# When and where sixteen weight tiles are decoded in a fused attention, gated MoE and channel-mixing kernel

## The chip, the cores and the metric

One core of a Trainium2 chip runs one program. The metric is the device time of one execution in microseconds (us), the median of several runs. Less is better. TensorE multiplies matrices (PE in the profile, PEld for its weight loads), VectorE (DVE), ScalarE (ACT) and GpSimd (POOL) work element by element, and SyncE (SP) issues transfers (DMAs) from one in-order queue.

## The reference

All arithmetic is float32; the weights `w_in`, `w_out`, `w_ch1`, `w_ch2` (and the small `conv_w`, `U`, `V`) arrive as float64.

```
x = attention(q, k, v, s)                 # 4 batches x 8 heads, 576 tokens, causal, exp, then P @ v
h = relu(x @ w_in)                        # 512 -> 1024, first MoE
x = (h * sigmoid(conv3(h))) @ w_out       # 1024 -> 512
u = x + (x.T @ U @ V).T                   # token mixing, rank 32
out = u + relu(u @ w_ch1) @ w_ch2         # 512 -> 2048 -> 512, second MoE
```

## The kernel before

**Arithmetic.** A float32 product is made of float32r matmuls on a high and a low part of each operand, three matmuls for one. The two big products of the second MoE use a Strassen scheme of seven products on halves (`WN`, `UN`, `VN`). The first, `u @ w_ch1`, is called the mixture here: 32 calls of `m2_in(f, g)`, where f is one of 8 pairs of row blocks and g one of 4 groups of tokens (PSUM tiles `ma`). The second, the last product of the program, is `m2_out` (tiles `my`).

**Weights.** A float64 tile of 128x512 is loaded as 512 KB into a buffer `raw` and decoded by `decode64`: one ACT instruction (line 538) and two DVE instructions (lines 545 and 554). The weights of the first MoE are done by head 11. After that two kinds of tiles go this way. `raw_w2a` are the tiles of `w_ch1`: `bring_w2a(f)` issues the loads of tiles f and f+8, `load_w2a(f)` decodes them and makes the seven high and low blocks, called W_f here, that `m2_in(f, ...)` multiplies with. `raw_w2b` are the 16 tiles of `w_ch2`: `keep_w2b` loads one, decodes it into `wf_w2b` and stores it (256 KB) to a DRAM scratch `w2b_d`, from which `load_w2b` reads it for the last product. All `raw` tiles share a ring of **two** buffers (`RINGS["w64"]`), so a load waits until the tile two before it is decoded. `wf_w2b` has a ring of two buffers too (three in the mixture), and a decode waits until the store of an earlier one has read its buffer.

**Stages.** (1) Attention over heads 0 to 31, in the loop `for h in range(NH + 1)`; from head 8 on the first MoE of the batch before is interleaved. (2) The first MoE of the last batch (`parts`), with W_0 and the u tiles prepared beside it. (3) The mixture, with W_1 to W_7 prepared about two blocks ahead. (4) The last product.

**What sets the order.** Every operation is recorded with an engine, a cost and the buffers that it reads and writes. `Plan.order` plays the program through with these costs and writes out each engine's instructions in the order in which they started there. The real engines run those orders, in order, and wait for data by semaphores. A transfer issued at t is booked to land at `max(wire, t + 1400) + bytes / 360 + 980 + slack` ns: 3.84 us later for an unhindered load of 512 KB with slack 0. If it lands later than booked, the instruction that needs it waits at the head of its engine's queue, with everything behind it.

**The 16 `keep_w2b` before:** one each at heads 13 to 17 and 23 to 27 (`W2B_AT`), where `keep_next` in the attention loop records it ahead of the parts of the first MoE; the other six in the mixture, after the calls with f = 1 and 2, g = 2 and 3, and after the first two with f = 3. Their order is tile 0, 8, 1, 9, 2, 10, and so on (`order2`). The store of a tile is recorded by the `keep_next` after it.

Of the kernel before, what the change touches and what calls it, by code (L numbers as in the profile page):

```python
# [60 lines left out]

FG = [(5, 0), (6, 0), (5, 1), (7, 0), (6, 1), (7, 1), (5, 2), (6, 2), (5, 3), (6, 3), (7, 3), (7, 2)]
EARLY2 = 8
W2B_AT = (13, 14, 15, 16, 17, 23, 24, 25, 26, 27)
OUT_AT = {0: "o11", 18: "o22", 22: "o21", 28: "o12"}
LAG2 = 6

# [3 lines left out]
WIRE = 1500  # L71
# [264 lines left out]
def tile_attention_moe_mixer(  # L336
# [14 lines left out]
    nc = tc.nc  # L351
# [13 lines left out]
    def dma(nbytes, fn, r, w):  # L365
        return plan.op("SP", 640, fn, r, w, late=nbytes / 360)
# [776 lines left out]
    def load_w2a(f, pool_):  # L1143

        blk = pool_.buf("W", [128, 2 * 7 * 256], F32R, f"W{f}")
        ws_[f] = blk

        def at(i, n, part):
            return lambda: blk[:, part * 1792 + 256 * i : part * 1792 + 256 * (i + n)]

        def keys(i, n, part):
            return [(blk, WN[j] + "hl"[part]) for j in range(i, i + n)]

        def decode(i):
            w = ring(dec, "wf", RINGS["wf"], [128, 512], F32, f"wf_w2a{f}_{i}")
            decode64(lambda: w(), [w], st["w2a", f][i], 512)
            return w

        def split(i, n, src, r):
            hi_act(at(i, n, 0), src, [r], keys(i, n, 0), 256 * n)  # L1160
            lo_dve(at(i, n, 1), src, at(i, n, 0), [r, *keys(i, n, 0)], keys(i, n, 1), 256 * n)

        def add(o, oi, x, y, op, r):
            dve(
                256,
                lambda: nc.vector.tensor_tensor(o[:, oi : oi + 256], x(), y(), op),
                r,
                [(o, oi)],
            )

        def part(t, i):
            return lambda: t[:, i : i + 256]

        wa = decode(0)
        split(0, 2, lambda: wa(), wa)
        yield
        wb = decode(1)
        split(2, 1, part(wb, 256), wb)
        yield
        sa, sb = (ring(w2a, "tt", RINGS["tt"], [128, S], F32, f"{n}_{f}") for n in ("S12", "S34"))  # L1180
        add(sa, 0, part(wb, 0), part(wb, 256), ALU.add, [wb])
        add(sa, 256, part(sa, 0), part(wa, 0), ALU.subtract, [(sa, 0), wa])
        split(3, 2, lambda: sa[:, 0:512], sa)
        yield
        add(sb, 0, part(wa, 0), part(wb, 0), ALU.subtract, [wa, wb])
        add(sb, 256, part(wa, 256), part(sa, 256), ALU.subtract, [wa, (sa, 256)])
        split(5, 2, lambda: sb[:, 0:512], sb)
        yield
# [72 lines left out]
    stores = []  # L1261

    def keep_w2b(ff):

        r = ring(dec, "raw", RINGS["w64"], [128, 512], I64, f"raw_w2b{ff}")
        dma(524288, lambda: nc.sync.dma_start(out=r(), in_=w2[ff][:, 512:]), [], [r])
        at = (w2a, "tt", RINGS["tt"], [128, S]) if st.get("mixed") else (dec, "wf", RINGS["wf"], [128, 512])
        w = ring(*at, F32, f"wf_w2b{ff}")
        decode64(lambda: w[:, :512], [w], r, 512)

        def store():
            o = dma(262144, lambda: nc.sync.dma_start(out=w2b_t[ff], in_=w[:, :512]), [w], [w2b_d[ff]])
            o.preds.add(next(x for x in reversed(plan.ops) if x.eng == "PE"))

        stores.append(store)

    def keep_next(more=True):
        while stores:
            stores.pop()()
        if order2 and more:  # L1280
            keep_w2b(order2.pop(0))

    def load_w2b(p):

        blk = w2_[p]
        r = ring(dec, "raw", RINGS["w64"], [128, 1024], F32, f"wb{p}")
        wa, wb = (Part(r, lambda t, a=a: t[:, a : a + 512], f"wb{p}_{a}") for a in (0, 512))
        for w, ff in ((wa, p), (wb, p + 8)):
            dma(262144, lambda w=w, ff=ff: nc.sync.dma_start(out=w(), in_=w2b_t[ff]), [w2b_d[ff]], [w])

        def at(i, n, part):
            return lambda: blk[:, part * 1792 + 256 * i : part * 1792 + 256 * (i + n)]

        def keys(i, n, part):
            return [(blk, VN[j] + "hl"[part]) for j in range(i, i + n)]

        def split(i, n, src, r):
            hi_act(at(i, n, 0), src, [r], keys(i, n, 0), 256 * n)
            lo_dve(at(i, n, 1), src, at(i, n, 0), [r, *keys(i, n, 0)], keys(i, n, 1), 256 * n)

        def add(o, oi, x, y, op, r):
            dve(256, lambda: nc.vector.tensor_tensor(o[:, oi : oi + 256], x(), y(), op), r, [(o, oi)])

        def part(t, i):
            return lambda: t[:, i : i + 256]

        split(0, 1, part(wa, 0), wa)
        yield
        split(1, 2, lambda: wb(), wb)
        yield  # L1310
        sa, sb = (ring(w2a, "tt", RINGS["tt"], [128, S], F32, f"{n}_b{p}") for n in ("S12", "S34"))
        add(sa, 0, part(wa, 256), part(wb, 256), ALU.add, [wa, wb])
        add(sa, 256, part(sa, 0), part(wa, 0), ALU.subtract, [(sa, 0), wa])
        split(3, 2, lambda: sa[:, 0:512], sa)
        yield
        add(sb, 0, part(wa, 0), part(wa, 256), ALU.subtract, [wa])
        add(sb, 256, part(wb, 0), part(sa, 256), ALU.subtract, [wb, (sa, 256)])
        split(5, 2, lambda: sb[:, 0:512], sb)
        yield
# [228 lines left out]
    for h in range(NH + 1):  # L1548
        b, hh = divmod(h - 1, H)
        todo = []  # L1550
        if b >= 1:
            parts = m1_parts(b - 1)
            whole = sum(w for w, t in parts)
            at, todo = 0, []
            for w, t in parts:
                if hh <= at * H / whole < hh + 1:
                    todo.append(t)
                at += w
        att_head(h)
        if h in W2B_AT or stores:  # L1560
            keep_next(h in W2B_AT)
        for n, (f, c) in enumerate(w1_jobs):
            if h == W1_AT[n]:
                load_split(w1[f], w1h[f, c], w1l[f, c], c, 512, f"w1_{f}_{c}", lo_dve, SLACK)
        if h == CW_AT:
            load_cw()
        if h == MIX_AT:
            load_mixu()
            for c in (0, HS):
                load_mixv(c)  # L1570
        for t in todo:
            t()

    w2a = Pool(plan, "w2a", "right", after=[ap.close()])

# [13 lines left out]

    st["late"] = True  # L1590

    bring_w2a(0)
    blocks = [u_block(w2a, 0)]
    steps = each(load_w2a(0, w2a), load_u(0, blocks[0])())
    parts = m1_parts(B - 1)
    for n, (w, t) in enumerate(parts):
        if n >= len(parts) // 3 and n % 2:
            next(steps, None)
        t()
# [36 lines left out]
    for dt in range(KT):  # L1636
        keep(B - 1, dt)

    m2_in(0, 2)
    m2_in(0, 3)  # L1640
    for f in (1, 2):
        bring_w2a(f + 2)
        steps = load_w2a(f + 2, pools[(f + 2) % 3])
        for g in (2, 3):
            next(steps)
            next(steps)
            m2_in(f, g)
            keep_next()
    for f in (3, 4):
        bring_w2a(f + 2)  # L1650
        steps = load_w2a(f + 2, pools[(f + 2) % 3])
        for g in range(NG):
            next(steps)
            m2_in(f, g)
            if order2 or stores:
                keep_next()
    bring_w2a(7)
    steps = load_w2a(7, pools[7 % 3])
# [36 lines left out]
    for i, (f, g) in enumerate(FG):  # L1695
        if i < 4:
            next(steps)
        m2_in(f, g)
        if f == 7 and g < 2:
            blk = (w2a, u1p)[g].buf(f"u{g}", [128, 2 * 7 * S], F32, f"w2_{g}")  # L1700
            add_w2(2 * g, blk, 0)
            add_w2(2 * g + 1, blk, 3584)
            pair(blk, 7168)
        elif f == 7:
            blk = u2p.buf(f"u{g}" + "a" * (g - 2), [128, (14 if g == 2 else 8) * S], F32, f"w2_{g}")
            add_w2(9 - g, blk, 0)
            if g == 3:
                pair(blk, 3584)
                blk = u2p.buf("u3b", [128, 6 * S], F32, "b21")
                b21 = [Cell(blk, k * NC2) for k in range(9)]  # L1710
            else:
                for k in range(5):
                    pair(blk, 3584 + 2 * k * NC2)
        elif g == 3:
            add_w2(f - 1, w_block(f, f"w2_W{f}"), 0)
        if i == 8:
            for ff in range(8):
                m2_bring(0, ff, "11")
# [114 lines left out]
```

## Time and the profile before

| | |
|---|---|
| median of 3 runs | 801.37 us (800.07 to 802.52) |
| the profiled execution | 799.74 us, span of its instructions 797.9 us |
| PE busy | 768.7 us, 96% of the span |
| DVE, ACT, POOL busy | 581.5 (73%), 526.0 (66%), 185.2 us (23%) |
| DMA | 132.84 MB, mean 166 GB/s |

PE is busy in almost every slice of the span, so time can come only from the stretches in which it sits idle or runs at a lower clock. Matmuls are pipelined, and busy time counts the overlap of two once. The time in brackets at the end of a timeline row is the idle time of that engine ahead of the instruction, with what ended it.

### The profile page before, as it was taken

How to read it: one execution, taken by the hardware profiler on the slowest of the kernel's cores; microseconds unless marked ns; L12 is line 12 of the kernel's file. 1: busy time of each engine (PE TensorE's matmuls, PEld its weight loads, DVE VectorE, ACT ScalarE, POOL GpSimd, SP SyncE). 2: the span in 40 equal slices, each digit the busy share in tenths (PEclk: the TensorE clock that was granted, in tenths of full speed). 3: DMA queues.
4: the chain of work that ended last, by engine and by line, in shares of the span. 5: the costliest groups of instructions: out<-in, count | busy, mean ns of one | idle time of the engine just before them, and what ended most of it. 6: DMA issues, size and time to landing. Idle time of an engine off the chain costs nothing.

```text
span 797.9 us, 15829 instructions
## 1 busy us (share of the span) xinstructions
PE 768.7 (96%) x5348; PEld 714.8 (90%) x5348; DVE 581.5 (73%) x1406; ACT 526.0 (66%) x1328; POOL 185.2 (23%) x291
## 2 busy tenths in 40 slices
PE   5999999899999989999999999999999999999998
PEld 3557797798889978999999999999999899999997
DVE  5987897536774458736789875567487998988983
ACT  4889998657887568966777644455456676656542
POOL 2565554553545334341230000000000000000000
PEclk9999999999999999999999999999999999999999
DMA  6578659663667636603043455886555968567121
GB/s 169 177 214 245 182 145 263 176 165 86 189 153 177 178 77 162 160 1 113 32 142 122 166 166 166 263 282 212 160 191 182 303 188 270 167 200 224 50 81 60
DMA packets 77257, 132.84 MB, mean 166 GB/s; under 512 B 10100, under 2 KB 52468, under 8 KB 77176
## 3 DMA queue, kind: packets, MB, share of 16 engines
q1 hardware_dynamic: 77104, 131.81, 56.4%
q8 instruction: 42, 0.69, 0.4%
q14 instruction: 39, 0.32, 0.1%
q10 hardware_dynamic: 72, 0.01, 0.0%
HBM read 77.72 MB, written 33.10 MB: 139 GB/s over the span
## 4 chain that ended last, share of the span: by engine, by line
PE 79%; DVE 8%; DMA 6%; issue 3%; ACT 2%; SPq 1%; POOL 1%; DVEq 0%; POOLq 0%; ACTq 0%
PE ma_A L1206 15%; PE my_X L1401 12%; PE y L953 11%; PE h L911 10%; PE ma_S L1206 6%; PE my_Y L1401 5%; PE sc L718 5%; PE pt L841 5%; PE av L867 5%; PE my_Z L1401 2%; DMA w2b_d<-wf_w2b 1%; DMA qkA<-t 1%; PE t L989 1%; DMA qkF<-cc 1%; DVE sc L679 1%
## 5 line engine op out<-in xcount | busy, mean ns | idle before, releaser
L953 PE MATMUL y<-gh,w1o 128*128 128x288 f32 x512 | 114.2, 300 | 0.1
L1206 PE MATMUL ma_A<-u,W 128*128 128x288 f32 x720 | 106.0, 295 | 0.0
L1206 PEld LDWEIGHTS ma_A<-u,W 128*128 128x128 f32 x720 | 99.4, 188 | 0.2
L707 POOL TENSOR_SCALAR P<-P,sm 128x128 f32<-128x128 f32 (+3 forms) x128 | 75.4, 606 | 96.8 <-DVE sm L770 86.7
L679 DVE CUSTOM_DVE_ANT_0 sc<-sc,mask 128x128 f32<-128x128 f32 (+2 forms) x144 | 69.1, 498 | 31.3 <-PE sc L718 27.6
L953 PEld LDWEIGHTS y<-gh,w1o 128*128 128x128 f32 x512 | 85.6, 188 | 1.0 <-DVE c L932 0.3
L392 POOL TENSOR_TENSOR gl<-c,gh 128x288 fp32r<-128x288 f32 x64 | 54.7, 862 | 118.9 <-ACT gh L938 107.5
L911 PE MATMUL h<-xh,w1h 128*128 128x290 f32 x256 | 79.9, 312 | 0.0
L923 DVE SCALAR_TENSOR_TENSOR c<-h,cw,c 128x288 f32<-128x288 f32 x128 | 64.2, 513 | 20.2 <-ACT c L919 19.1
L911 PE MATMUL h<-xl,w1h 128*128 128x290 f32 x256 | 76.3, 298 | 0.0
L911 PE MATMUL h<-xh,w1l 128*128 128x290 f32 x256 | 76.2, 298 | 0.0
L1220 ACT COPY s<-ma_A 128x288 f32<-128x288 f32 x96 | 37.9, 398 | 58.1 <-PE ma_A L1206 51.0
L953 PE MATMUL y<-gl,w1o 128*128 128x288 f32 x256 | 75.3, 294 | 0.0
L696 ACT ACTIVATE P<-sc,sm 128x128 f32<-128x128 f32 (+3 forms) x128 | 67.7, 534 | 7.5 <-DVE sm L679 7.4
L380 ACT COPY th<-pt 128x384 f32<-128x384 f32 (+2 forms) x128 | 63.1, 494 | 8.3 <-PE pt L841 7.3
L380 ACT CAST w<-b 128x384 fp32r<-128x384 f32 x88 | 44.2, 513 | 33.6 <-PE my_X L1401 15.0
L841 PE MATMUL pt<-ident,P 128*128 128x128 f32 x320 | 60.0, 275 | 2.3 <-ACT h L917 1.3
L1401 PE MATMUL my_X<-w,w 128*128 128x384 f32 x324 | 60.3, 334 | 0.1
L1401 PEld LDWEIGHTS my_X<-w,w 128*128 128x128 f32 x324 | 56.4, 188 | 0.5 <-DVE w L389 0.5
L867 PE MATMUL av<-th,vr 128*64 128x320 f32 (+4 forms) x448 | 50.7, 366 | 0.7 <-ACT th L380 0.7
L389 DVE TENSOR_TENSOR w<-b,w 128x384 fp32r<-128x384 f32 x88 | 46.9, 554 | 5.2 <-ACT w L380 3.9
L911 PEld LDWEIGHTS h<-xh,w1h 128*128 128x128 f32 x256 | 48.4, 189 | 2.3 <-ACT P L696 0.8
(208 smaller groups left out, 1923.8 us busy)
## 6 DMA issues: line engine op xcount, KB each, us to landing
b<-ch_d SPq DMA_DIRECT2D x96, 192.0 KB
ch_d<-s SPq DMA_DIRECT2D x64, 144.0 KB
raw_w<-w_in SPq DMA_DIRECT2D x16, 512.0 KB
raw_w2b<-w_in SPq DMA_DIRECT2D x16, 512.0 KB
raw_w2a<-w_in SPq DMA_DIRECT2D x16, 512.0 KB
t<-qk_in SPq DMA_DIRECT2D x24, 288.0 KB
qkB<-t SPq DMA_DIRECT2D x24, 288.0 KB
qkA<-t SPq DMA_DIRECT2D x24, 288.0 KB
```

The lines of the kernel that those rows point to most:

```text
L380: act(n, lambda: nc.scalar.copy(out(), src()), r, w)
L392: pool(n, lambda: nc.gpsimd.tensor_tensor(out(), src(), f32(hi()), ALU.subtract), r, w, two=True)
L679: lambda: nc.vector.tensor_tensor_reduce(out=ps[:rows, :w], in0=ps[:rows, :w], in1=mask[:rows, m0 : m0 + w], scale=-0.125, scalar=3.0e38 i ...
L696: lambda: nc.scalar.activation(out(), ps[:rows, :w], ACTF.Exp, bias=low(), scale=-1.0, accum_out=total()),
L707: lambda: nc.gpsimd.tensor_scalar(t[:, :w], t[:, :w], r(), 1.0, ALU.mult, ALU.mult),
L841: nc.tensor.transpose(pt[:, o + rows - 128 : o + rows], d["P"][i][:, 128 * j : 128 * j + 128], turn)
L867: nc.tensor.matmul(ps[64 * e : 64 * e + 64, o:n], lhsT=vr[:, e, j, :], rhs=t[:, pos[j] : pos[j] + w], start=c == 0, stop=c == len(ops) - 1 ...
L911: nc.tensor.matmul(ps[:, :W], lhsT=ww, rhs=xx, start=kt + n == 0, stop=kt == KT - 1 and n == 2)
L923: lambda k=k: nc.vector.scalar_tensor_tensor(c(), hh[:, k : k + HS], cw[:, 3 * f + k : 3 * f + k + 1], c(), ALU.mult, ALU.add),
L953: nc.tensor.matmul(ps[:, :HS], lhsT=ww, rhs=xx(), start=f + n == 0, stop=f == NF1 - 1 and n == 2)
L1206: nc.tensor.matmul(ps[:, :HS], lhsT=ww, rhs=uu, start=first and k == 0, stop=k == 5, skip_group_check=True)
L1401: nc.tensor.matmul(ps[:, :NC2], lhsT=ww, rhs=xx(), start=first and k == 0, stop=f == 7 and k == 2, skip_group_check=True,)
```

## The change

The decodes at heads 13 to 17 and 23 to 27 go. Six tiles (0, 8, 1, 9, 2, 10) are kept in the loop passes h = 30 (one), 31 (two) and 32 (three; that pass has no head of its own any more), spread between the parts of the first MoE. The other ten are kept after calls of the mixture: two with f = 0 and two with each of f = 1 to 4. Load, store and re-load of these tiles are booked with `slack = WIRE`, 1500 ns. In `load_w2a` the second half of W_f is decoded ahead of the split of the first. `W2B_LAST` is empty, so the loop over `parts` starts W_0 at its first pass; its new lines are left out here.

```diff
-W2B_AT = (13, 14, 15, 16, 17, 23, 24, 25, 26, 27)
+W2B_AT = {30: 1, 31: 2, 32: 3}
+W2B_MA = {(0, 2): 1, (0, 3): 1, (1, 2): 1, (1, 3): 1, (2, 2): 1, (2, 3): 1, (3, 1): 1, (3, 2): 1, (4, 1): 1, (4, 2): 1}
+W2B_LAST = ()
...
         wa = decode(0)
+        wb = decode(1)
         split(0, 2, lambda: wa(), wa)
         yield
-        wb = decode(1)
         split(2, 1, part(wb, 256), wb)
...
-        dma(524288, lambda: nc.sync.dma_start(out=r(), in_=w2[ff][:, 512:]), [], [r])
+        dma(524288, lambda: nc.sync.dma_start(out=r(), in_=w2[ff][:, 512:]), [], [r]).slack = WIRE
...
             o = dma(262144, lambda: nc.sync.dma_start(out=w2b_t[ff], in_=w[:, :512]), [w], [w2b_d[ff]])
+            o.slack = WIRE
...
-        if h in W2B_AT or stores:
-            keep_next(h in W2B_AT)
...
-        for t in todo:
+        keeps, done = W2B_AT.get(h, 0), 0
+        if stores:
+            keep_next(False)
+        for n, t in enumerate(todo):
+            while done < keeps and done * len(todo) <= n * keeps:
+                keep_next()
+                done += 1
             t()
+        for _ in range(done, keeps):
+            keep_next()
...
             m2_in(f, g)
-            keep_next()
+            for _ in range(W2B_MA.get((f, g), 0)):
+                keep_next()
```

No instruction is added or removed on any engine; what moves is the order. In the rows of the change below, L numbers are two to three higher than those of the same line before.

On ACT, at head 16 of the attention (P16 is its probabilities, c0_1_7 a gate of the first MoE), before:

```order
L696 ACTIVATE P16_1_2162,sm_0_175<-sc16_1_2138,sm_0_175 128x256
L696 ACTIVATE P16_2_2168,sm_0_175<-sc16_2_2144,sm_0_175 128x384
L538 ACTIVATE raw_w2b2_2113<-raw_w2b2_2113 128x512
L929 ACTIVATE c0_1_7_2147<-c0_1_7_2147 128x288
L696 ACTIVATE P16_3_2200,sm_0_175<-sc16_3_2159,sm_0_175 128x512
```

On ACT at the same place, in the change:

```order
L698 ACTIVATE P16_1_2140,sm_0_175<-sc16_1_2111,sm_0_175 128x256
L931 ACTIVATE c0_1_7_2109<-c0_1_7_2109 128x288
L698 ACTIVATE P16_2_2157,sm_0_175<-sc16_2_2115,sm_0_175 128x384
L698 ACTIVATE P16_3_2165,sm_0_175<-sc16_3_2132,sm_0_175 128x512
L940 CAST gh0_1_7_2184<-c0_1_7_2109 128x288
```

The decode of tile 2 no longer stands between the softmax of head 16 and the gate.

On SP, the two loads of W_3 (raw_w2a3 and raw_w2a11) stood before among the first stores of the mixture (ch_d is the scratch of its results, p2_0_0 the first result of f = 0, g = 0):

```order
L1139 DMA raw_w2a3_5992<-w2_in 128x512
L1231 DMA ch_d0_78<-p2_0_0_5981 128x288
L1139 DMA raw_w2a11_6014<-w2_in 128x512
L1231 DMA ch_d8_86<-c2_0_0_6081 128x288
L1231 DMA ch_d0_78<-p2_0_1_6095 128x288
```

On SP, in the change, they stand among the stores of f = 0, g = 2 and 3:

```order
L1141 DMA raw_w2a3_6533<-w2_in 128x512
L1233 DMA ch_d0_78<-s7_0_2_6531 128x288
L1233 DMA ch_d8_86<-s6_0_2_6461 128x288
L1233 DMA ch_d0_78<-p2_0_3_6550 128x288
L1141 DMA raw_w2a11_6570<-w2_in 128x512
```

They moved behind tiles 3 and 11 of `w_ch2`, which now take both `raw` buffers first.

On DVE, the second half of W_7, the last block of the mixture (S12 and S34 are sums of its two halves, c2_4_3 a result of `m2_in(4, 3)`), stood before at:

```order
L554 SCALAR_TENSOR_TENSOR wf_w2a7_1_7494<-raw_w2a15_7402,wf_w2a7_1_7494 128x512
L1166 TENSOR_TENSOR S12_7_7507<-wf_w2a7_1_7494 128x256
L1166 TENSOR_TENSOR S34_7_7517<-wf_w2a7_0_7437,wf_w2a7_1_7494 128x256
L1166 TENSOR_TENSOR S12_7_7507<-S12_7_7507,wf_w2a7_0_7437 128x256
L1166 TENSOR_TENSOR S34_7_7517<-wf_w2a7_0_7437,S12_7_7507 128x256
L1224 TENSOR_TENSOR c2_4_3_7533<-ma4_3_S3_7485,s5_4_3_7528 128x288
```

On DVE, in the change, it stands at:

```order
L556 SCALAR_TENSOR_TENSOR wf_w2b15_7568<-raw_w2b15_7420,wf_w2b15_7568 128x512
L391 TENSOR_TENSOR W7_7564<-wf_w2a7_0_7544,W7_7564 128x512
L1226 TENSOR_TENSOR p2_6_0_7591<-ma6_0_A12_7557,p1_6_0_7570 128x288
L1226 TENSOR_TENSOR c2_5_0_7602<-ma5_0_S3_7534,s5_5_0_7589 128x288
L1226 TENSOR_TENSOR s6_5_0_7555<-ma5_0_S3_7534,s6_5_0_7555 128x288
L1226 TENSOR_TENSOR c2_6_0_7640<-ma6_0_S3_7593,s5_6_0_7637 128x288
L547 TENSOR_SCALAR wf_w2a7_1_7651<-raw_w2a15_7587 128x512
L1226 TENSOR_TENSOR p2_5_1_7660<-ma5_1_A12_7642,p1_5_1_7649 128x288
L556 SCALAR_TENSOR_TENSOR wf_w2a7_1_7651<-raw_w2a15_7587,wf_w2a7_1_7651 128x512
L1226 TENSOR_TENSOR s6_6_0_7600<-ma6_0_S3_7593,s6_6_0_7600 128x288
L1168 TENSOR_TENSOR S12_7_7680<-wf_w2a7_1_7651 128x256
```

It moved from the results of `m2_in(4, 3)` to those of `m2_in(6, 0)`, behind the decode of the last tile of `w_ch2` (w2b15), whose `raw` buffer its load takes over.

## Rows read from the trace of the kernel before

**Rows 1.** Windows: busy (instructions) of PE, PEld, DVE, ACT, POOL; granted clock, DMA share, GB/s.

```profile
120.00:180.00 60.00, 56.06 (x412) 49.71 (x411) 32.06 (x101) 40.18 (x116) 30.09 (x50) 0.97 0.75 199
...
300.00:345.00 45.00, 45.00 (x347) 41.34 (x345) 32.23 (x97) 36.65 (x103) 17.84 (x28) 1.00 0.56 143
345.00:430.00 85.00, 85.00 (x643) 82.92 (x642) 61.70 (x123) 60.22 (x144) 23.32 (x33) 1.00 0.20 68
430.00:562.00 132.00, 131.61 (x983) 130.55 (x982) 91.26 (x199) 69.46 (x159) 0.00 (x0) 1.00 0.65 211
```

**Rows 2.** Timeline of PE from 120 to 300 us: instructions behind its longest gaps.

```profile
132.10 0.44 PE L867 MATMUL av<-th,vr 128*64 128x256 f32 x2 [0.66 <-ACT th L380]
...
156.63 0.33 PE L841 MATMUL pt<-ident,p 128*128 128x128 f32 x1 [2.90 <-DVE c L932]
...
222.57 0.33 PE L718 MATMUL sc<-qkB 128*128 128x128 f32 x1 [0.65 <-DVE c L932]
...
282.73 0.33 PE L841 MATMUL pt<-ident,p 128*128 128x128 f32 x1 [1.33 <-ACT P L696]
...
296.40 0.39 PE L718 MATMUL sc<-qkB 128*128 128x256 f32 x1 [0.66 <-DVE c L932]
```

**Rows 3.** Timeline of SP, ACT and DVE ahead of the longest of them.

```profile
149.19 0.71 SPq L1266 DMA_DIRECT2D raw_w2b<-w_in  x1
149.95 0.67 SPq L1272 DMA_DIRECT2D w2b_d<-wf_w2b  x1
...
155.11 0.66 ACT L538 ACTIVATE raw_w2b<-raw_w2b 128x512 f32<-128x512 f32 x1 [3.64 <-DMA raw_w2b<-w_in]
...
155.75 0.43 DVE L545 TENSOR_SCALAR wf_w2b<-raw_w2b 128x512 int32<-128x512 int32 x1 [3.58 <-DMA w2b_d<-wf_w2b]
```

**Rows 4.** Waits from 120 to 300 us: us in total, times, longest.

```profile
ACT raw_w2b L538 <- DMA raw_w2b<-w_in: 10.1, 5, 3.6
DVE wf_w2b L545 <- DMA w2b_d<-wf_w2b: 8.6, 3, 3.6
```

**Rows 5.** Windows behind the longest gap, columns as in the first group.

```profile
157.60:161.00 3.40, 3.40 (x19) 2.87 (x16) 1.33 (x8) 2.25 (x7) 3.40 (x7) 0.51 0.00 0
161.00:164.40 3.40, 3.40 (x30) 2.44 (x29) 2.23 (x6) 2.18 (x8) 2.21 (x3) 0.99 0.44 94
```

**Rows 6.** One decode: engine, count, ns min/median/max, first and last start.

```profile
L538 ACT ACTIVATE raw_w2b<-raw_w2b x16: 657/678/711, 127.5 to 526.1; 128x512 f32<-128x512 f32 x16
L545 DVE TENSOR_SCALAR wf_w2b<-raw_w2b x16: 418/426/444, 128.7 to 526.8; 128x512 int32<-128x512 int32 x16
L554 DVE SCALAR_TENSOR_TENSOR wf_w2b<-raw_w2b,wf_w2b x16: 681/688/874, 129.6 to 527.5; 128x512 int32<-128x512 int32 x16
```

**Rows 7.** Waits from 430 to 562 us, columns as in group 4.

```profile
ACT raw_w2a L538 <- DMA raw_w2a<-w_in: 4.7, 4, 1.5
...
DVE p L1224 <- DMA raw_w2a<-w_in: 3.6, 1, 3.6
...
PE ma_S L1206 <- DVE s L1224: 0.4, 1, 0.4
```

**Rows 8.** Timeline of SP and ACT: one load of the mixture and its decode.

```profile
526.32 0.33 SPq L1139 DMA_DIRECT2D raw_w2a<-w_in  x1
...
531.33 0.67 ACT L538 ACTIVATE raw_w2a<-raw_w2a 128x512 f32<-128x512 f32 x1 [1.35 <-DMA raw_w2a<-w_in]
```

**Rows 9.** Windows with the most DMA, columns as in the first group.

```profile
500.00:540.00 40.00, 39.61 (x298) 39.38 (x297) 25.35 (x57) 21.20 (x49) 0.00 (x0) 1.00 0.84 269
620.00:640.00 20.00, 18.25 (x99) 16.65 (x98) 18.23 (x40) 11.40 (x24) 0.00 (x0) 1.00 0.93 302
```

**Rows 10.** Timeline of DVE and PE: p2_6_0, W_7's last split, its S products.

```profile
552.94 0.46 DVE L1224 TENSOR_TENSOR p<-ma_A,p 128x288 f32<-128x288 f32 x1 [0.26 <-issue]
553.32 0.68 DVE L389 TENSOR_TENSOR W<-S,W 128x512 fp32r<-128x512 f32 x1
...
565.09 0.83 PE L1206 MATMUL ma_A<-u,W 128*128 128x288 f32 x5
```

More of the change, by code (lines that the diff above doesn't have):

```diff
@@ L1288, in load_w2b @@
         for w, ff in ((wa, p), (wb, p + 8)):
-            dma(262144, lambda w=w, ff=ff: nc.sync.dma_start(out=w(), in_=w2b_t[ff]), [w2b_d[ff]], [w])
+            dma(262144, lambda w=w, ff=ff: nc.sync.dma_start(out=w(), in_=w2b_t[ff]), [w2b_d[ff]], [w]).slack = WIRE
         def at(i, n, part):
@@ L1590, in tile_attention_moe_mixer @@
     st["late"] = True
-    bring_w2a(0)
     blocks = [u_block(w2a, 0)]
-    steps = each(load_w2a(0, w2a), load_u(0, blocks[0])())
+    steps = None
     parts = m1_parts(B - 1)
     for n, (w, t) in enumerate(parts):
+        if n in W2B_LAST:
+            keep_next()
+        if n > max(W2B_LAST, default=-1) and steps is None:
+            while stores:
+                stores.pop()()
+            bring_w2a(0)
+            steps = each(load_w2a(0, w2a), load_u(0, blocks[0])())
         if n >= len(parts) // 3 and n % 2:
@@ L1637, in tile_attention_moe_mixer @@
         keep(B - 1, dt)
-    m2_in(0, 2)
-    m2_in(0, 3)
+    for g in (2, 3):
+        m2_in(0, g)
+        for _ in range(W2B_MA.get((0, g), 0)):
+            keep_next()
     for f in (1, 2):
@@ L1647, in tile_attention_moe_mixer @@
             m2_in(f, g)
-            keep_next()
+            for _ in range(W2B_MA.get((f, g), 0)):
+                keep_next()
     for f in (3, 4):
@@ L1654, in tile_attention_moe_mixer @@
             m2_in(f, g)
-            if order2 or stores:
+            for _ in range(W2B_MA.get((f, g), 0)):
                 keep_next()
@@ L1698, in tile_attention_moe_mixer @@
         m2_in(f, g)
+        if (f, g) in W2B_MA or stores:
+            keep_next((f, g) in W2B_MA)
         if f == 7 and g < 2:
@@ L1723, in tile_attention_moe_mixer @@
             more(4)
-    assert not order2 and not stores
+    assert not order2 and not stores, (order2, len(stores))
     c6 = sn.close()
```

## Prediction

> **What bounds the kernel now.** I read the windows by stage first. In the stretches of 300 to 430 us PE is busy all of the time, and in the mixture, 430 to 562 us, all but 0.4 us of 132; from 120 to 180 us it is idle for 3.9 of 60 [rows 1]. ScalarE and VectorE always have spare time, so the program is bound by PE, and a change of order can give back only idle time or lost clock of PE.
>
> Then the timeline of PE, for its gaps between 120 and 300 us, the stretch of the heads from 9 to 27. There are five over 0.5 us: 0.66, 2.90, 0.65, 1.33 and 0.66 us, together 6.2 us [rows 2]. Each names a softmax or gate instruction of ACT or DVE as what ended it, which is not the cause. The timeline of the other engines shows that. The load of tile 2 was issued at 149.19, the ACT half of its decode stood at the head of ACT's queue until 155.11, 3.64 us, and the DVE half waited for 3.58 us for a store of an earlier tile, issued at 149.95, to leave its buffer [rows 3]. The softmax of head 16 stands behind both, and PE waits for it. By the waits of this stretch ACT stood for such loads five times (10.1 us) and DVE for such stores three times (8.6 us) [rows 4]; each of the five PE gaps follows one of these waits by at most 6 us. I found no other transfer that ACT or DVE wait for in this stretch.
>
> The longest gap costs twice. Right behind it the granted clock is 0.51, half of the 2.4 GHz level, for 3.4 us, and PE starts 19 matmuls in that time against 30 in the same time after [rows 5]. At half the clock 3.4 us do the work of 1.7; by the count, 11 matmuls of 3.4 / 30 us, it is 1.25 us. I take 1.5. Behind the four shorter gaps the clock stays up.
>
> **The change part by part.** *What goes from the heads.* Ten decodes, each 0.68 us of ACT and 0.43 + 0.69 us of DVE [rows 6], lie beside PE and give nothing by themselves. With them go the waits: 6.2 us of gaps and 1.5 us of clock, **-7.7 us**. It would be less if the softmax chain had another late input behind this one; the waits show none. The bounds are -6.2 (the clock gives nothing back) and -7.9.
>
> *Six decodes in passes 30 to 32.* From 300 to 345 us ACT is busy for 36.7 of 45 us and DVE for 32.2 [rows 1], more than in the stretch that loses the decodes. Four ACT halves (2.7 us) come here, and two of W_0 (1.4 us) leave to a later place, since W_0's loads now wait for buffers. So ACT still has 7 us to spare, and DVE no less than before. The loads of tiles 0 and 8 stand on SP well ahead of their decodes; a load took 5.9 us from issue to release [rows 3]. Tiles 2 and 10 and W_0 come between 345 and 430 us, where DVE is busy for 61.7 of 85 us and ACT for 60.2. There W_0's loads are issued only as these tiles leave the ring, and they carry no slack: booked at 3.84 us, landing after 5.0 to 5.9 [rows 3, 8], so ACT and DVE wait up to 2 us twice. PE is in a long run of `y` products then, whose operands are ready. Bounds: nothing, and six times what a decode costs in the heads (7.7 / 10), 4.6. Nearer to nothing: **+0.7**.
>
> *Ten decodes in the mixture instead of six.* This is the nearest measured case: there ACT already waits for loads of W for 4.7 us and DVE once for 3.6, and PE loses one gap of 0.4 us in all [rows 7]. PE has eight PSUM buffers to run ahead into. Four more decodes add 2.7 us of ACT and 4.5 us of DVE to 69.5 and 91.3 of 132 [rows 1]. What is new is where the W loads stand. The ring of two buffers makes W_3 wait for tiles 3 and 11, and W_7 for tile 15. W_3 has room: by the order PE needs it only after all of f = 2. W_7 is the narrow place. Before, its last split ends at 553.32 + 0.68 = 554.0 and its S products start in the row at 565.09 [rows 10], 11 us later. In the change tile 15's decode ends just ahead of p2_6_0, at about 552.5 [rows 10]; only then can the load of W_7's second half go out. With 5.0 to 5.9 us to land [rows 3, 8] it is there at 557.5 to 558.4. Then follow 0.68 us of ACT, 1.11 of DVE, four sums of at most 0.46, a cast of at most 0.7 and a split of 0.68 [rows 6, 10]: 5.0 us, so 562.5 to 563.4 if nothing stands between. The S products stand 12 matmuls (1.6 us) earlier in the new order, at about 563.9. The 11 us of cover shrink to about 1, and results of `m2_in(5, 0)` and `(6, 0)` stand between. Bounds of the mixture: -0.4 (its gap goes) and ten times 0.77, 7.7. The measured mixture is near the lower end; with W_7's risk I take **+1.0**.
>
> *The slack of 1500 ns* only places consumers later. It would cover a wait of 1.5 us, not the worst one of 3.6. *The earlier second decode* in `load_w2a` and *the later re-loads of `w2b`* I cost at nothing: what hides them is PE's supply of products of the block before; without it a decode is 1.8 us [rows 6].
>
> The rule of the Trainium skill that bears on the loads is in DMA: Bandwidth & Descriptors, Anatomy of one DMA: a transfer takes about 2.0 us and its bytes at 436 GB/s (measured there for transfers issued by GpSimd). For 512 KB that would be 3.2 us, an estimate from that page, less than the 3.84 booked; the waits above would not exist. The trace disagrees with 5.0 to 5.9 us, and the measurement decides. By the page the mixture would cost nothing and the sum below would come to 794.4; I give that 0.05, inside the chance of the forecast.
>
> **Sum.** 799.74 - 7.7 + 0.7 + 1.0 = 793.7 us for an execution like the profiled one. The median of the runs is 801.37, 1.6 us above it, so I expect a median of **795.4 us**.
>
> **Rivals.** *The stalls move with the decodes.* The same sixteen loads land as late as before, in two rings of two buffers, only elsewhere. For it: the waits for W in the mixture exist already. Against it: with 8.3 us of such waits there PE lost 0.4 [rows 7]. If each moved decode cost 0.5 to 0.8 us, as in the heads, 5 to 8 us come back: 799 to 803.8, no change that can be told.
>
> *W_7 and its like arrive too late (slower).* If the second half of each of W_4 to W_7 reaches PE later than needed, PE stands still at the start of f. It becomes slower by more than 2.4 us once those four blocks cost more than 7.7 - 0.7 + 2.4 = 9.4 us, about 2.3 us each, and gaps of the size of 2.90 would bring the halved clock along. Transfers speak for it: from 500 to 540 us the engines are busy for 0.84 at 269 GB/s, and where they are at 0.93 (302 GB/s, 620 to 640 us) PE already starves, 18.25 of 20 us [rows 9]. Two more loads of 0.5 MB fall into those 40 us, 26 GB/s more, so 295 GB/s. Against it: by the order W_4 to W_6 are needed well after their decodes, a whole block of products later. That gives 804 to 808.
>
> *A part only.* Heads 30 to 32, where ACT has the least room, or W_7, take 2 to 4 us: 797.5 to 799.
>
> **How the numbers follow.** The forecast, 793 to 797.5, has 0.60; a part only 0.12; the stalls move, 799 to 803.8, 0.16; slower 0.09; better than 793, 0.03, if the gap of the mixture goes too and the transition to the last product happens to start better. What a measurement of this kernel can tell from no change is about 0.3%, 2.4 us: faster means below 799.0. So faster 0.75, same 0.16, slower 0.09. The range to hold eight in ten, 792.5 to 802.0, takes in the part and most of the moved stalls; the likeliest case alone is 793 to 797.5.
>
> **What would show it.** Right: PE has no gap over 0.5 us between 120 and 300 us, no wait of ACT or DVE for `raw_w2b` or `w2b_d` is in that stretch, and the granted clock there stays at the 2.4 GHz level. From 300 to 430 us PE gaps stay under 1 us in sum. In the mixture ACT waits for `raw_w2a` grow, PE gaps stay under 1.5 us, and W_7's last split ends 0 to 3 us ahead of its S products. Wrong: gaps of PE at the first product with W_7 or W_3, with DVE `W` as what ended them; a halved clock after 430 us; or gaps in the heads that another input of the softmax leaves.

## The result and the profile after

The median fell from 801.94 us (800.07 to 804.77, 4 runs) to **792.19 us** (790.48 to 792.8, 4 runs): a ratio of 0.9872, 95% interval 0.9838 to 0.9906. It is faster, as forecast, but by 9.75 us where 6.0 were forecast, and the median lies 0.3 us below the range.

The profiled execution took 792.8 us (span 791.0). To see which stage the time came from I counted PE's matmuls: both traces list 5348, and between the same two counts lies, but for a few at the edges, the same work. The cuts, counted from 0, are the 600th (in head 8, ahead of the first place where PE's order differs), the 2956th (last products of the first MoE), the 4340th (end of the mixture) and the last. At the 4340th the edges differ: 12 matmuls of the last product stand ahead of it in the changed kernel and 6 before; they are longer than those of the mixture (0.17 against 0.13 us each), so some 0.2 us pass from one stage to the other by the cut alone.

| us | to 600 | heads and first MoE | mixture | last product | median (lowest to highest) |
|---|---|---|---|---|---|
| before | 99.9 | 321.0 | 185.9 | 179.2 | 801.94 (800.07 to 804.77) |
| changed | 102.0 | 311.2 | 190.2 | 176.4 | 792.19 (790.48 to 792.80) |
| y_changed (the same again) | 103.5 | 311.2 | 188.7 | 176.5 | 792.67 (789.88 to 794.72) |
| x1_book | 105.8 | 315.0 | 186.3 | 176.5 | 793.30 (791.06 to 797.30) |
| x7_book4 | 101.0 | 312.7 | 185.8 | 176.2 | 790.71 (788.88 to 792.37) |
| x11_book4early | 104.3 | 312.3 | 185.4 | 176.6 | 791.63 (789.82 to 792.41) |
| x2_place | 106.8 | 311.0 | 190.3 | 179.1 | 793.97 (793.19 to 800.37) |
| x3_reload | 100.7 | 311.2 | 187.6 | 179.5 | 792.39 (792.30 to 793.26) |
| x5_w2a | 103.0 | 311.1 | 188.7 | 177.3 | 792.56 (791.87 to 793.25) |
| x4_second | 103.3 | 311.1 | 186.4 | 176.2 | 790.25 (786.96 to 795.49) |
| y_second (the same again) | 104.2 | 311.1 | 186.9 | 176.2 | 790.84 (787.32 to 794.97) |
| x12_secondreload | 107.1 | 311.1 | 185.8 | 178.8 | 792.43 (788.30 to 796.22) |
| x8_six | 100.9 | 311.4 | 194.8 | 177.8 | 798.26 (797.28 to 800.75) |
| x10_sixsecond | 102.1 | 311.5 | 195.1 | 178.1 | 798.51 (797.04 to 800.25) |

The stages are each of one profiled execution. The change won 9.8 us in the heads and 2.8 in the last product, and lost 4.2 in the mixture: 8.4 net. The first 600 matmuls, which it doesn't touch, came out 2.1 us longer, which leaves 6.3; what lies ahead of the first matmul and behind the last gives the other 0.6 of the span's 6.9.

**Heads.** The timeline of PE lists no gap over 0.25 us between 115 and 300 us where before it has those of [rows 2], and the waits of [rows 4] are gone there. The windows of the changed kernel (columns as in [rows 1]):

```profile
120.00:180.00 60.00, 59.91 (x463) 54.06 (x463) 33.49 (x109) 43.22 (x128) 28.36 (x50) 1.00 0.59 143
300.00:345.00 45.00, 44.87 (x343) 40.83 (x344) 31.82 (x97) 36.39 (x105) 20.61 (x30) 1.00 0.50 142
345.00:421.00 76.00, 76.00 (x573) 74.16 (x572) 59.92 (x115) 54.97 (x125) 21.31 (x27) 1.00 0.34 110
```

The first row has 463 matmuls in 60 us where 412 were, and no lost clock. In the other two, where six decodes now stand, PE is idle for 0.13 us.

**Mixture.** Waits of the changed kernel from 421 to 609 us (us in total, times, longest):

```profile
ACT raw_w2a L540 <- DMA raw_w2a<-w_in: 11.9, 9, 2.2
...
ACT s L1222 <- DMA ch_d<-s: 5.6, 5, 1.7
...
PE ma_A L1208 <- ACT s L1222: 1.2, 2, 1.0
...
PE ma_S L1208 <- DVE c L1226: 1.2, 1, 1.2
```

ACT's waits for W loads went from 4.7 us [rows 7] to 11.9. How late transfers reach PE is seen in the timeline of ACT, of DVE beside it, and of PE behind them:

```profile
523.04 0.68 ACT L540 ACTIVATE raw_w2b<-raw_w2b 128x512 f32<-128x512 f32 x1
525.58 0.67 ACT L540 ACTIVATE raw_w2a<-raw_w2a 128x512 f32<-128x512 f32 x1 [1.87 <-DMA raw_w2a<-w_in]
527.21 0.70 ACT L1222 COPY s<-ma_A 128x288 f32<-128x288 f32 x2 [0.96 <-DMA ch_d<-s]
...
541.47 0.52 ACT L1338 ACTIVATE b_x<-b_x 128x384 f32<-128x384 f32 x1 [1.70 <-DMA b_x<-ch_d]
541.90 0.38 ACT L1222 COPY s<-ma_A 128x288 f32<-128x288 f32 x1
```

```profile
526.29 0.43 DVE L547 TENSOR_SCALAR wf_w2a<-raw_w2a 128x512 int32<-128x512 int32 x1 [1.38 <-ACT raw_w2a L540]
526.63 0.45 DVE L1226 TENSOR_TENSOR s<-ma_S,s 128x288 f32<-128x288 f32 x1
...
542.31 0.46 DVE L1226 TENSOR_TENSOR c<-ma_S,s 128x288 f32<-128x288 f32 x1 [1.81 <-DMA b_xth<-ch_d]
```

```profile
527.66 3.46 PE L1208 MATMUL ma_A<-u,W 128*128 128x288 f32 x24 [1.02 <-ACT s L1222]
...
542.82 0.40 PE L1208 MATMUL ma_S<-u3a,W 128*128 128x288 f32 x1 [1.23 <-DVE c L1226]
```

The copies `s`, which empty PSUM buffers for PE, stand in ACT's queue behind the decode, and the decode waits for its load. PE has run ahead by then and stops for 1.02 us until the copy at 527.21 has made room. That copy waited for 0.96 us more: the row names the store of an earlier `s`, and DVE's `s` at 526.63, which stood behind the DVE half of the same decode, ended within 0.03 us of it. In y_changed, the same kernel again, this copy waits for DVE `s` by its row (0.92 us), and PE stops for 0.77 us. The longer gap, 1.23 us at 542.82, has another load as its cause: ACT stood for 1.70 us for `b_x`, an operand of the last product that is fetched ahead, with the copy `s` of 541.90 behind it. DVE's `c` waits for ACT and began 0.03 us after this copy ended (the load that its row names landed at the same moment), and PE waited for `c`. So W loads make a part of the gaps, not all of them. On SP the W load of the first of these gaps was issued at:

```profile
519.42 0.42 SPq L1141 DMA_DIRECT2D raw_w2a<-w_in  x1
```

From there to its release at 525.58 are 6.2 us, against 3.84 booked. The Trainium skill (DMA: Bandwidth & Descriptors, Anatomy of one DMA) gives, for transfers that GpSimd issues, a fit that comes to 3.2 us for 512 KB, an estimate from that page; the trace, with SP as the issuer, has 6.2 us here.

### The profile page after: what moved, and what is told of

It reads as the page before. It is cut to its first block, busy times and chain, and to the rows that moved or that the text cites. A ratio compares the mean times of both kernels' runs of the same rounds, so it can differ in the third digit from the quotient of the medians.

```text
span 791.0 us, 15838 instructions
## 1 busy us (share of the span) xinstructions
PE 768.0 (97%) x5348; PEld 714.2 (90%) x5348; DVE 582.3 (74%) x1406; ACT 528.3 (67%) x1328; POOL 185.6 (23%) x291
## 4 chain that ended last, share of the span: by engine, by line
PE 76%; DMA 8%; DVE 8%; ACT 4%; issue 2%; SPq 1%; POOL 0%; DVEq 0%; ACTq 0%
PE y L955 13%; PE h L913 11%; PE my_X L1404 11%; PE ma_A L1208 10%; PE sc L720 6%; PE my_Y L1404 5%; PE pt L843 5%; PE av L869 5%; PE ma_S L1208 4%; DMA raw_w2a<-w_in 2%; PE my_Z L1404 2%; DMA b<-ch_d 1%; PE tp L972 1%; DMA ch_d<-s 1%; PE t L991 1%
## 5 line engine op out<-in xcount | busy, mean ns | idle before, releaser
L1208 PE MATMUL ma_A<-u,W 128*128 128x288 f32 x720 | 106.8, 296 | 1.1 <-ACT s L1222 1.0
```

Of the source, the lines that this page charges most:

```text
L1208: nc.tensor.matmul(ps[:, :HS], lhsT=ww, rhs=uu, start=first and k == 0, stop=k == 5, skip_group_check=True)
```

## The experiments

The theory: the five gaps of the heads came from transfers that land later than booked, ahead of which ACT and DVE stood, and the change pays part of it back in the mixture. Rivals: the decode work itself made the gaps; booking alone, or placement alone, is the whole of it; the rest is order and chance.

### x1_book: the kernel before with the three slacks alone

```diff
-        dma(524288, lambda: nc.sync.dma_start(out=r(), in_=w2[ff][:, 512:]), [], [r])
+        dma(524288, lambda: nc.sync.dma_start(out=r(), in_=w2[ff][:, 512:]), [], [r]).slack = WIRE
...
+            o.slack = WIRE
...
-            dma(262144, lambda w=w, ff=ff: nc.sync.dma_start(out=w(), in_=w2b_t[ff]), [w2b_d[ff]], [w])
+            dma(262144, lambda w=w, ff=ff: nc.sync.dma_start(out=w(), in_=w2b_t[ff]), [w2b_d[ff]], [w]).slack = WIRE
```

> The kernel before with the three slacks of 1500 ns alone (load, store and re-load of the w2b tiles); the decodes stay in heads 13 to 27. If waits for transfers that were booked too early make the head gaps (my theory), a slack of 1.5 us covers a part of waits of 1 to 3.6 us: PE gaps from 115 to 300 us fall from 7.0 to some 1 to 4 us, and the kernel is 3 to 6 us faster than before. If the decode work of ACT and DVE among the softmax makes them (rival), the gaps stay at 6 to 7 us and the time within 1.5 us of before. If booking is the whole of it (second rival), the gaps go to under 0.5 us, and with the later re-loads the kernel reaches the changed kernel's time or less, 788 to 792 us.

Measured: 0.9876 of before (0.9838 to 0.9915). The waits that 1.5 us covers only in part are still there from 120 to 300 us:

```profile
DVE wf_w2b L545 <- DMA w2b_d<-wf_w2b: 4.7, 2, 3.8
ACT raw_w2b L538 <- DMA raw_w2b<-w_in: 3.4, 4, 1.4
```

They were 8.6 and 10.1 us [rows 4]. PE's gaps from 115 to 300 us fell from 7.0 to 3.3 us and the stage by 6.0, as the theory of waits has it. The decodes still stand there, so their work did not make most of the gaps. Of the 3.3 us left, half has another late transfer as its cause, a transfer of the attention's q and k, which the theory does not name:

```profile
PE sc L718 <- DMA qkA<-t: 1.7, 2, 1.4
```

Not expected: the last product got 2.7 us shorter, which makes this kernel nearly as fast as the changed one without any decode moved.

### x7_book4: slack above the longest wait

```diff
-        dma(524288, lambda: nc.sync.dma_start(out=r(), in_=w2[ff][:, 512:]), [], [r])
+        dma(524288, lambda: nc.sync.dma_start(out=r(), in_=w2[ff][:, 512:]), [], [r]).slack = 4000
...
+            o.slack = 4000
```

Against the kernel before; the re-loads have 1500 as in x1.

> The kernel before with slack of 4000 ns on load and store of the w2b tiles and 1500 ns on the re-loads; decodes stay in heads 13 to 27, and the mixture keeps its six. 4000 ns is more than the longest wait of the heads, 3.64 us. Theory of the waits: PE gaps from 115 to 300 us under 1 us and no halved clock there, the mixture as cheap as before (0.4 us), so 8 us faster than before and 1 to 4 us faster than the changed kernel. Rival, the decode work itself: gaps stay at 5 us or more, time as before.

Measured: 0.984 of before (0.9808 to 0.9872), 790.71 us. Windows of the heads:

```profile
120.00:180.00 60.00, 59.59 (x457) 53.38 (x455) 37.76 (x115) 45.37 (x132) 30.03 (x50) 1.00 0.77 203
180.00:300.00 120.00, 119.56 (x907) 109.10 (x906) 77.53 (x222) 91.47 (x255) 52.28 (x85) 1.00 0.61 154
```

PE is idle for 0.85 of the 180 us with all ten decodes in their old places, and the stage is 8.4 us shorter than before. So the waits cost 8.4 us. What is left to the changed kernel is 312.7 - 311.2 = 1.5 us (1.1 by x11). It is not shown to be the price of the decode work: PE is idle for 0.6 us more than in the changed kernel there, 0.3 of it for `qkA<-t` again, and x8 below, which has all ten decodes in this stage too, but in passes 28 to 32, takes 311.4 us. The mixture stays at 185.8 us, as it had to.

### x2_place: placement without slack

```diff
-        dma(524288, lambda: nc.sync.dma_start(out=r(), in_=w2[ff][:, 512:]), [], [r]).slack = WIRE
+        dma(524288, lambda: nc.sync.dma_start(out=r(), in_=w2[ff][:, 512:]), [], [r])
...
-            o.slack = WIRE
...
-            dma(262144, lambda w=w, ff=ff: nc.sync.dma_start(out=w(), in_=w2b_t[ff]), [w2b_d[ff]], [w]).slack = WIRE
+            dma(262144, lambda w=w, ff=ff: nc.sync.dma_start(out=w(), in_=w2b_t[ff]), [w2b_d[ff]], [w])
```

> The changed kernel without its three slacks: only the places of the decodes are changed. By my theory the heads are free of gaps as in the changed kernel (the decodes are gone from there), and waits for raw_w2b and for stores come back in passes 30 to 32 and in the mixture: 0 to 5 us slower than the changed kernel, 793 to 797 us. If the entry to the last product gained by the later re-loads, its PE gaps go back from 0.8 to some 2.7 us. If the booking were the whole of the gain, this kernel would be near the time of before, 799 us or more.

Measured: 0.9895 of before (0.9858 to 0.9933). The heads are as free as in the changed kernel and the last product is back at 179.1 us. The waits for `raw_w2b` come back in the mixture (ACT 6.9 us; DVE 4.4 us for stores), but its time of 190.3 us is the changed kernel's: with or without them, something else sets it. Neither booking nor placement is the whole; each removes the heads' waits by itself (booking with the 4000 ns of x7), so their gains don't add.

### x8_six and x10_sixsecond: six decodes in the mixture

```diff
-W2B_AT = {30: 1, 31: 2, 32: 3}
-W2B_MA = {(0, 2): 1, (0, 3): 1, (1, 2): 1, (1, 3): 1, (2, 2): 1, (2, 3): 1, (3, 1): 1, (3, 2): 1, (4, 1): 1, (4, 2): 1}
+W2B_AT = {28: 2, 29: 2, 30: 2, 31: 2, 32: 2}
+W2B_MA = {(1, 2): 1, (1, 3): 1, (2, 2): 1, (2, 3): 1, (3, 0): 1, (3, 1): 1}
```

x10 also has the second decode back at its old place, the edit of x4 below.

> The changed kernel with ten decodes in heads 28 to 32, two in each, and only six in the mixture, at the places where the kernel before had its six. It prices the four decodes more in the mixture. If these cost the 2.6 us that the PE gaps of the mixture grew by, gaps there go back to 0.4 to 1 us and the kernel is 1 to 3 us faster than the changed one, if heads 28 to 32 take four more decodes with under 0.5 us of gaps. If the mixture's gaps come of the other order and transfers rather than of the number, they stay at 2 to 3 us and the time within 1 us.

> The kernel with ten decodes in heads 28 to 32 and six in the mixture, with the second decode of a W block back behind the first split. With the earlier second decode its mixture took 194.8 us and PE stood still for 4.2 us once, behind a sum for W that waited for a store of a w2b tile. If the earlier second decode is what makes it, the mixture falls to 186 to 187 us and the kernel to 789 to 791 us. If it is the store booked later and the shared ring of tt buffers, the long gap stays and the mixture is at 192 us or more.

Measured: 0.9943 (0.9919 to 0.9966) and 0.9955 (0.9942 to 0.9969) of before, some 6 us slower than the changed kernel. I was wrong: the mixture got longer. The timeline of x8 on SP, DVE, ACT and PE:

```profile
522.43 0.68 DVE L556 SCALAR_TENSOR_TENSOR wf_w2b<-raw_w2b,wf_w2b 128x512 int32<-128x512 int32 x1
...
546.92 0.66 SPq L1274 DMA_DIRECT2D w2b_d<-wf_w2b  x1
...
549.46 0.43 DVE L1168 TENSOR_TENSOR S<-wf_w2a 128x256 f32<-128x256 f32 x1 [2.93 <-DMA w2b_d<-wf_w2b]
...
550.38 1.29 ACT L382 CAST W<-S 128x512 fp32r<-128x512 f32 x2 [3.07 <-DVE S L1168]
...
551.04 0.85 PE L1208 MATMUL ma_A<-u,W 128*128 128x288 f32 x2 [4.22 <-ACT W L382]
```

The sums for W and the decodes of w2b share the ring `tt`; here a sum waits for a store that goes out late, the cast of W waits for the sum, and PE for W. The granted clock behind the gap is halved (columns as in [rows 1]):

```profile
551.00:557.80 6.80, 6.38 (x25) 6.03 (x26) 5.32 (x13) 2.96 (x6) 0.00 (x0) 0.50 0.55 177
557.80:564.60 6.80, 6.80 (x53) 6.80 (x53) 5.12 (x13) 2.52 (x6) 0.00 (x0) 1.00 0.46 153
```

25 matmuls against 53 in the same time. Of the 8.9 us by which this mixture is longer than before, one late W costs 4.2 and half of 6.8, 7.6 us. x10 shows the same gap of 4.19 us, so the second decode is not its cause.

The edit does more than it was meant to. In the kernel before, `keep_next` follows every `m2_in` of f = 3 and 4 as long as a store is left to record. In the changed kernel it follows them only where `W2B_MA` has an entry; for a store that is left over, the next one comes after `m2_in(5, 0)`. In x8 and x10 the last entry is (3, 1), so the last tile, decoded by 523.1, keeps its `tt` buffer until its store at 546.92, 24 us later. In x1 and x7, with the same six places, its store is issued 0.1 to 0.2 us after its decode. These two runs therefore do not price the four decodes more in the mixture; they show what a store recorded late does.

### x3_reload: the changed kernel without slack on the re-loads

```diff
-            dma(262144, lambda w=w, ff=ff: nc.sync.dma_start(out=w(), in_=w2b_t[ff]), [w2b_d[ff]], [w]).slack = WIRE
+            dma(262144, lambda w=w, ff=ff: nc.sync.dma_start(out=w(), in_=w2b_t[ff]), [w2b_d[ff]], [w])
```

> The changed kernel without the slack on the re-loads of w2b alone. The runs so far say that this slack, not the move, shortens the last product: from the 4340th matmul to the end the kernel took 179.2 us before, 176.4 changed, 176.5 with booking alone and 179.1 with placement alone. If so, this kernel is 2 to 3 us slower than the changed one there (178.5 to 179.5) and the same ahead of it. Rival: it is the store's or the load's slack, or the order that the move brings: then that stretch stays at 176.4.

Measured: 0.9892 of before (0.9874 to 0.991). The last product is at 179.5 us, as expected, but the mixture is 2.6 us shorter, and the whole time the same. Since the changed kernel run again had 188.7 us, 1.5 less than its first profile, more than half of this counter-movement lies within what executions differ by; x12 repeats the edit where the mixture has fewer gaps.

### x4_second and y_second: the second decode back behind the first split; y_changed: no edit

```diff
         wa = decode(0)
-        wb = decode(1)
         split(0, 2, lambda: wa(), wa)
         yield
+        wb = decode(1)
         split(2, 1, part(wb, 256), wb)
```

> The changed kernel with the second decode of a W block back behind the first split. The mixture (2956th to 4340th matmul) took 185.9 us before and 190.2 changed. If the earlier second decode makes the mixture's new gaps, because it holds ACT and DVE up for the second load while the first half could be split, the mixture falls to 186 to 187.5 us and the kernel gains 3 us. If the four decodes more and the ring of two buffers make them, it stays at 189 to 191.

> The changed kernel with the second decode back behind the first split, once more, beside the changed kernel on one chip: its first runs went from 787.0 to 795.5. If its mixture of 186.4 us, 3.7 less than the changed kernel's, is real, the stage comes out at 186 to 187 again and the median 2.5 to 4 us under the changed kernel's, 788 to 790.5. If it was chance, stage and median are within 1 us of the changed kernel's.

> The changed kernel once more, beside its variants on one chip, since the medians of the variants lie within each other's spread. By the stages of its first profile: 311.2 us from the 600th to the 2956th matmul, 190.2 to the 4340th, 176.4 to the end, each again within 0.7 us; the first 600 matmuls anywhere from 100 to 107. Median 791 to 793.5.

Measured: 0.9861 (0.9834 to 0.9889) and, run again, 0.9845 (0.9807 to 0.9883) of before; the changed kernel on the chip of y_second 0.9861 (0.9828 to 0.9894). The mixture took 186.4 and 186.9 us, against 190.2 and 188.7. Waits of x4 in its mixture, 416 to 605 us:

```profile
ACT raw_w2a L540 <- DMA raw_w2a<-w_in: 3.6, 5, 1.5
...
PE ma_A L1208 <- ACT s L1222: 0.5, 2, 0.3
```

11.9 us of ACT's waits are 3.6, in y_second 4.6 (changed again: 11.5). By stages the early second decode costs 1.8 to 3.7 us; the medians show 1.8 to 1.9, less than I expected, and their ranges overlap. That it costs is shown, how only in part. My account was that ACT goes to stand for the second load while it could split the first half; but of the 11.9 us 5.3 are waits for first halves (0.3 in x4) and 6.6 for second ones (3.3 in x4), so the edit moves more than the one wait.

### x11_book4early: the early second decode beside six decodes

The kernel x7_book4 with one edit more:

```diff
         wa = decode(0)
+        wb = decode(1)
         split(0, 2, lambda: wa(), wa)
         yield
-        wb = decode(1)
```

> The kernel before with slack of 4000 ns on load and store in the heads, and the earlier second decode as the one edit more. Without it the mixture took 185.8 us, with its six decodes. If the earlier second decode costs by itself, the mixture goes up by 2 to 4 us to 188 to 190; if it costs only with ten decodes and their loads around it, it stays under 187, as it made no difference beside six decodes with the ten in heads 28 to 32 (194.8 against 195.1).

Measured: 0.9847 of before (0.9813 to 0.9881); the mixture took 185.4 us, and ACT waited 3.5 us for W loads. By itself the early decode costs nothing that shows. It costs beside the ten decodes of the changed kernel; why there is not shown. A later second load is not the reason: it goes out 6.2 us after the first in the changed kernel, the mean of W_1 to W_7, and 9.2 us after it here.

### x5_w2a: slack on the loads of W

```diff
-            dma(524288, lambda r=r, ff=ff: nc.sync.dma_start(out=r(), in_=w2[ff][:, :512]), [], [r])
+            dma(524288, lambda r=r, ff=ff: nc.sync.dma_start(out=r(), in_=w2[ff][:, :512]), [], [r]).slack = WIRE
```

> The changed kernel with a slack of 1500 ns on the loads of W (raw_w2a) too, the only loads of the mixture that have none. If the waits of ACT for W loads booked too early make the mixture's gaps, ACT waits for raw_w2a fall under 0.5 us and the mixture from 190.2 to 186 to 188 us. If the loads are late whatever they are booked at, because the ring gives their buffers late, it stays at 189 to 191 or gets longer.

Measured: 0.9889 of before (0.9871 to 0.9907). ACT's waits for W loads are gone altogether, but the mixture took 188.7 us: now W itself is late, with a PE gap of 0.67 us ended by DVE `W`. Later booking turns a wait of ACT into a wait for W, and the last product begins worse (177.3). No gain: the mixture is as long as in y_changed, where ACT waits 11.5 us for W loads, so these waits alone do not set its time.

### x12_secondreload: both edits

The changed kernel with the edits of x4 and x3:

```diff
-        wb = decode(1)
         split(0, 2, lambda: wa(), wa)
         yield
+        wb = decode(1)
...
-            dma(262144, lambda w=w, ff=ff: nc.sync.dma_start(out=w(), in_=w2b_t[ff]), [w2b_d[ff]], [w]).slack = WIRE
+            dma(262144, lambda w=w, ff=ff: nc.sync.dma_start(out=w(), in_=w2b_t[ff]), [w2b_d[ff]], [w])
```

> The changed kernel with the second decode back behind the first split and no slack on the re-loads: what the re-load slack is worth where nothing else disturbs the mixture. If it is worth 2.8 to 3 us in the last product, that stretch takes 179 us or more, against 176.2 with it, the mixture 186 to 187, and the kernel is 2.5 to 3 us slower than the same without this edit. If the mixture gets as much shorter as it did in the changed kernel (190.2 to 187.6), it goes to 184 us; 185.5 is what its matmuls take without gaps, so that this can't be.

Measured: 0.9856 of before (0.9816 to 0.9897). Mixture 185.8, last product 178.8 us: the latter is 2.6 us more than in x4 and y_second, the former 0.6 to 1.1 us less, of which the cut makes 0.2. By medians it is 1.6 to 2.2 us slower. In the last product the re-load slack is thus worth 2.6 to 3.1 us (x12, x3, and changed against x2), for the whole kernel less: 1.6 to 2.2 us by the medians of x12, and 0.2 by that of x3.

What moves with it is seen on SP around the start of the last product. Before:

```profile
601.31 0.80 SPq L1289 DMA_DIRECT2D wb<-w2b_d  x2
...
609.97 0.82 SPq L1289 DMA_DIRECT2D wb<-w2b_d  x2
...
613.26 0.32 SPq L1329 DMA_DIRECT2D b<-ch_d  x1
```

Changed:

```profile
597.75 0.80 SPq L1292 DMA_DIRECT2D wb<-w2b_d  x2
...
603.35 0.80 SPq L1292 DMA_DIRECT2D wb<-w2b_d  x2
...
607.13 0.32 SPq L1332 DMA_DIRECT2D b<-ch_d  x1
```

The last re-loads wait on SP for the DVE split that frees their buffer (before it ends at 609.94, changed at 603.33), and the first loads of `b`, the operands of the last product, stand behind them. The 4340th matmul starts at 614.52 and 610.76, so the first `b` goes out 1.3 us ahead of it before and 3.6 us changed. Without the slack (x2, x3, x12) it is 1.3 us and the last product takes 178.8 to 179.5 us; with it, in x1, x4, x7 and x11 and both runs of the changed kernel, 3.6 us and 176.2 to 176.6; x5 lies between with 2.1 us and 177.3. The slack does not bring this about in every order: x8 and x10 book it too, and there the first `b` goes out 1.3 us ahead and the last product takes 177.8 and 178.1 us. Nor is the lead shown to be all of it: at the same 1.3 us that stage takes from 177.8 to 179.5, and PE's own order changes as well (its first product of the last stage is the 4328th matmul instead of the 4310th). No run separates the two. ACT's waits for `b` (610 to 645 us before, 608 to 640 changed):

```profile
ACT b L1335 <- DMA b<-ch_d: 4.7, 5, 2.9
```

```profile
ACT b L1338 <- DMA b<-ch_d: 2.3, 4, 0.7
```

They are 3.3 us in y_changed and in x8, with last products of 176.5 and 177.8 us, so these waits by themselves do not give the stage's time.

## Why the prediction was right and wrong

**The bound and the cause: right.** PE's gaps in the heads came from waits for late transfers: they go when the waits go, with the decodes in place (x7) or away (x2). The clock stays up, and in the changed kernel no other input of the softmax stood behind; in x1 a transfer of q and k did, for 1.7 us.

**The first step that failed: the price of the heads' waits, -7.7.** The waits were worth 8.4 us (x7), and the move took 9.8 us off the stage. I added up the five gaps over 0.5 us, 6.2; all idle time of PE from 115 to 300 us was 7.0 before and is 0.2 in the changed kernel. With 1.5 for the clock that makes 8.3, and the other 1.5 us is in no row. A part of it can lie in how rows count: a run of 24 matmuls takes 3.46 us in the row above, 0.14 each, but the page of the changed kernel gives 296 ns as the mean of one, so by my estimate a stop costs up to 0.15 us more than the row shows as idle; no run tests this. That the ten decodes "give nothing by themselves" is not refuted: with all ten in this stage x8 takes 311.4 us, the changed kernel 311.2. Six decodes in passes 30 to 32, +0.7, cost nothing that shows. Together: -7.0 forecast, -9.8 measured.

**The mixture: right sign, wrong size and place.** +1.0 forecast, +4.2 (and, run again, +2.8) measured. W_7 held, by a narrow margin: its last split ended at 559.74 us, inside a run of 30 matmuls of PE that had begun at 557.48 and had no gap. PE's gaps over 0.25 us in the mixture came to 2.7 us where I had put under 1.5. What cost was the edit I "cost at nothing", the earlier second decode: 2.7 us of it, the mean of the five traces with it and ten decodes (189.1) less that of the three without (186.4). The four decodes more cost about 0.5 us (186.4 against 185.9). I had looked for the cover on PE's side, and not at the queues of ACT and DVE, where the copies and sums for PE stand behind an instruction that waits for a load, of W or of `b_x`.

**The second step that failed: the "later re-loads", also cost at nothing.** With them the last product took 2.8 us less (2.6 to 3.1 by the runs without their slack), though a part came back in the mixture: x3, without this slack, has a median of 792.39 us. I had the starved stretch at 620 to 640 us in a row [rows 9] and used it only as a warning; I never asked which loads stand ahead of `b` on SP.

**The sum.** With the measured terms, 799.74 - 9.8 + 4.2 - 2.8 = 791.3 where I had 793.7: the gap of 2.4 us is two gains missed (2.8 each) less a loss missed (3.2). That the forecast came out only 3.2 us too high (795.4 against 792.19) is luck, since these errors have opposite signs. The last 0.8 us is the step from one execution to the median, 1.6 by my sum and 0.9 here: the profiled execution of before was a lucky one, with the shortest first 600 matmuls of all fourteen, 99.9 us.

**Rivals.** Stalls that move with the decodes: in part, as above, but never near 5 us. W too late, with the halved clock behind it: not in the changed kernel, but x8 and x10 are that case, by a store recorded late and not by a late load, with 8.9 and 9.2 us more of mixture where I had put 9.4 as the point from which the kernel is slower; there the heads and the last product had gained more than I counted, and it stayed faster than before. A better start of the last product, to which I gave 0.03 together with a quieter mixture, came without the quieter mixture; together with the larger gain in the heads it carried the result below 793.

**The best version.** x4 (790.25 and 790.84 us) and x7 (790.71 us) lie under the changed kernel (792.19 and 792.67) in median and in sum of stages, but the intervals of the ratios overlap: that they beat it is likely and not shown. From the 600th matmul on, without the stretch that no edit touches, x4 took 673.7 and 674.1 us, x7 674.6, and the changed kernel 677.7 and 676.4. x7 moves no decode at all.

## What to carry to other kernels

Where an order is planned from booked times, compare issue to release in the trace with the booking first: a slack of 4000 ns on the loads and stores and of 1500 on the re-loads did here what moving ten decodes did. Cost every edit at the queue that it is in: what stands behind a waiting instruction on its engine, and behind a waiting transfer on SP, pays for it. And count work (matmuls done by a time) rather than idle time when stages of two traces are compared.

## What the hardware showed that I had not expected

The untouched first 600 matmuls took 99.9 to 107.1 us in fourteen profiled executions. Eight of them have one or two stretches at the lower clock there. In y_second, the timeline of PE ahead of one and the windows on it:

```profile
84.63 0.55 PE L843 MATMUL pt<-ident,P 128*128 128x128 f32 x3 [1.32 <-ACT h L919]
...
85.86 0.33 PE L843 MATMUL pt<-ident,P 128*128 128x128 f32 x1 [0.57 <-POOL P L709]
```

```profile
86.60:90.00 3.40, 3.40 (x17) 2.73 (x16) 1.85 (x5) 3.12 (x8) 2.16 (x3) 0.50 1.04 240
90.00:93.40 3.40, 3.40 (x28) 3.37 (x27) 2.45 (x7) 2.08 (x5) 0.19 (x1) 1.00 0.85 209
```

17 matmuls against 28. The granted clock of 0.50 is the level of 1.2 GHz. Wherever it fell ahead of the program's end, in all fourteen traces, it stayed there for 3.4 or 6.8 us, and PE had a gap of 0.96 to 4.22 us at that point or in the 2 us ahead of it. Not every such gap brings it: the 1.33 us of [rows 2] did not, nor one of 2.43 us in x12. The stretch took 99.9 to 103.0 us in the six traces without a fall in it, 102.1 to 104.3 in the five with 3.4 us of lowered clock, and 105.8 to 107.1 in the three with 6.8. Two executions of one kernel, changed and y_changed, differ by 1.5 us in this stretch and by another 1.5 in the mixture, so medians of kernels 2 us apart overlap.
